# The sums of a row block of the project pass on DVE instead of POOL, and loads four row blocks ahead

## The chip, the core and the metric

The kernel runs on one core of a Trainium2 chip. The metric is the device time of one execution in microseconds, the median of several runs.

## The reference

Three layers in a row over 8 x 576 positions, 512 channels wide, all in fp32: a retention attention without softmax, a feed-forward layer with token mixing, and a gated feed-forward layer. In the middle one, with `x` the first layer's result:

```python
xt = x.transpose(0, 2, 1)
h = xt @ U @ V
u = x + h.transpose(0, 2, 1)
ch = np.maximum(u @ w_ch1, 0.0) @ w_ch2
return (u + ch).astype(np.float32)
```

`w_ch1` is 512 x 2048, `w_ch2` 2048 x 512. The last layer mixes each position with the one before it, and multiplies `relu(xk @ w_k)**2 @ w_v` with a sigmoid of `xr @ w_r`.

## The kernel before, in words

Each fp32 operand of a product is split into a high part (a copy on ACT, rounded to the fp32r type, L363) and a low part (the difference, on DVE, L364); a product is three matmuls: high by high, low by high, high by low.

The text is about the **project pass**, `relu(u @ w_ch1) @ w_ch2`. The nine column blocks of 512 positions are taken in four pairs (q = 0 to 3; the ninth is done apart behind them). The product of a pair is not made of eight block products but of seven (numbered 1 to 7) of sums and differences of blocks. Products 2, 1, 7 and 5 are made in a first half (h = 0), 6, 4 and 3 in a second (h = 1). Each half runs over eight **row blocks** (j = 0 to 7) of the hidden dimension, so there are 64 row blocks, counted by n. A row block is 24 matmuls in a first half (L404) and 18 in a second, each with 128 x 512 moving data, accumulated in four groups of PSUM banks (`ga` to `gd`).

What a row block goes through, by function:

- `load_item`: two tiles of 128 x 2 x 512, `ra` and `rb`, are loaded from DRAM by SP's queue. In a first half both hold four blocks of the hidden layer `hp`; in a second half `rb` is loaded again, and `ra` takes a half tile from the DRAM scratch `t`.
- `sums_item`: two operations of 128 x 512 (L345 and L346 in a first half, L349 and L350 in a second) make the sums in place. In a first half one sum is stored to `t` for the second half (L347).
- `split_item`: `sah` and `sbh` on ACT, `sal` and `sbl` on DVE.
- `products`: the matmuls. Behind the last row block of a half, `leave_group` takes the PSUM groups out: copies on ACT (L418, L440), additions on DVE (L424, L444), and it puts closures into the list `rest`: additions on POOL (L421, L432, L435, L454) and DVE (L448). These add the residual `u` (tiles `ur`, loaded by `load_rest`), and each result `x2` is then stored (L380), with a copy of its last column on ACT (L379).

`ra`, `rb`, `sbl` and `ur` share one pool of 16 buffers, `big2`; a new tile waits for the last reader of the one whose buffer it takes. On each engine instructions run in the order in which the code records them, and SP's queue is in order as well: a transfer that waits holds those behind it. The loop over n records the load of n+3, the sums of n+2, the split of n+1, the products of n, and then one closure of `rest` in a second half and two in a first.

Of the kernel before, what the change touches and what calls it, by code (L numbers as in the profile page):

```python
# [15 lines left out]
ALU = mybir.AluOpType  # L16
# [23 lines left out]
def retention_mixer_kernel(ctx: ExitStack, tc: tile.TileContext, io):  # L40
    nc = tc.nc

    consts = ctx.enter_context(tc.tile_pool(name="consts", bufs=1))
    big = ctx.enter_context(tc.tile_pool(name="big", bufs=35))
# [11 lines left out]
    def unit(pool, dt, nm):  # L56
        return pool.tile([128, 2, 512], dt, tag="unit", name=nm)

    def small(dt, nm):
        return sm.tile([128, 512], dt, tag="small", name=nm)  # L60
# [264 lines left out]
    ITEMS = [(q, h, j) for q in range(NB // 2) for h in range(2) for j in range(NF // 2)]  # L325
# [3 lines left out]
    def load_item(n):  # L329
        q, h, j = ITEMS[n]  # L330
        ra[n] = unit(big2, F32, f"ra{n}")
        rb[n] = unit(big2, F32, f"rb{n}")
        if h == 0:
            nc.sync.dma_start(ra[n], hp[q][:, j, 0:2])
        else:
            nc.sync.dma_start(ra[n][:, 0], t1_blk[q][:, j])
        nc.sync.dma_start(rb[n], hp[q][:, j, 2:4])
# [3 lines left out]
    def sums_item(n):  # L341
        q, h, j = ITEMS[n]
        a, b = ra[n], rb[n]
        if h == 0:
            nc.gpsimd.tensor_tensor(b[:, 0], b[:, 0], a[:, 1], op=ALU.subtract)  # L345
            nc.gpsimd.tensor_tensor(a[:, 1], a[:, 1], a[:, 0], op=ALU.subtract)  # L346
            nc.sync.dma_start(t1_blk[q][:, j], a[:, 1])  # L347
        else:
            nc.gpsimd.tensor_tensor(a[:, 0], b[:, 0], a[:, 0], op=ALU.subtract)  # L349
            nc.gpsimd.tensor_tensor(b[:, 1], b[:, 1], a[:, 0], op=ALU.subtract)  # L350

    def split_item(n):
        q, h, j = ITEMS[n]
        a, b = ra.pop(n), rb.pop(n)
        x = {}
        for nm, src, where in (("a", a, big), ("b", b, big2)):
            hi = unit(big, F32R, f"s{nm}h{n}")
            lo = unit(where, F32R, f"s{nm}l{n}")
            if h == 1 and nm == "a":
                src, hi_, lo_ = src[:, 0], hi[:, 0], lo[:, 0]  # L360
            else:
                hi_, lo_ = hi, lo
            nc.scalar.copy(hi_, src)  # L363
            nc.vector.tensor_tensor(lo_, src, hi_.bitcast(F32), op=ALU.subtract)  # L364
            x[nm] = hi, lo
        parts_of[n] = x
# [3 lines left out]
    ur = {}  # L370
    rest = []

    def load_rest(q, who):
        t, o = 2 * q + who % 2, who // 2
        ur[who] = unit(big2, F32, f"ur{t}_{o}")
        nc.sync.dma_start(ur[who], u_blk[t][:, 2 * o:2 * o + 2, :])

    def done_x2(t, o, x):
        nc.scalar.copy(edge[:, o, t:t + 1], x[:, BT - 1:BT])  # L379
        nc.sync.dma_start(x2_blk[t][:, o, :], x)  # L380

    def products(n):
        q, h, j = ITEMS[n]
        x = parts_of.pop(n)

        if h == 0:
            plan = {
                1: ("a", wp, 0, "a", 0), 2: ("b", wp, 1, "b", 1),
                5: ("d", wp, 2, "a", 1), 7: ("c", wp, 3, "b", 0),
            }  # L390
            seq_ = (2, 1, 7, 5) if j == 0 else (1, 7, 5, 2)
        else:
            plan = {6: ("a", wq, 2, "a", 0), 4: ("c", wq, 1, "b", 1), 3: ("d", wq, 3, "b", 0)}
            seq_ = (6, 4, 3)
        last = j == NF // 2 - 1
        for m in seq_:
            g, w, wi, nm, xi = plan[m]
            if h == 0 and j == 0:
                group[g] = [bank(2 * "abcd".index(g) + p, f"g{g}{q}_{p}") for p in range(2)]
            wh, wl = (v[:, wi] for v in w[j])  # L400
            xh, xl = (v[:, xi] for v in x[nm])
            for p in range(2):
                for i, (l, r) in enumerate(((wh, xh), (wl, xh), (wh, xl))):
                    nc.tensor.matmul(  # L404
                        group[g][p], l[:, col(p)], r,
                        start=(h == 0 and j == 0 and i == 0),
                        stop=(i == 2 and last),
                        skip_group_check=True,
                    )
            if last:  # L410
                for p in range(2):
                    leave_group(q, m, p, group[g][p])

    def leave_group(q, m, p, ps):
        if m in (1, 5, 7):
            to = {1: m1, 5: m5, 7: m7}[m]
            to[p] = small(F32, f"m{m}_{q}_{p}")
            nc.scalar.copy(to[p], ps)  # L418
        elif m == 2:
            def first(x=None):  # L420
                nc.gpsimd.tensor_tensor(m1[p], m1[p], ur[0][:, p], op=ALU.add)  # L421

            def out():
                nc.vector.tensor_tensor(m1[p], ps, m1[p], op=ALU.add)  # L424
                done_x2(2 * q, p, m1[p])

            rest.insert(p, first)
            rest.append(out)
            if p == 1:
                for i in range(2):  # L430
                    def add(i=i):
                        nc.gpsimd.tensor_tensor(m7[i], m7[i], m5[i], op=ALU.add)  # L432

                    def add_u(i=i):
                        nc.gpsimd.tensor_tensor(m7[i], m7[i], ur[3][:, i], op=ALU.add)  # L435

                    rest.extend([add, add_u])
        elif m == 6:
            u2[p] = small(F32, f"u2_{q}_{p}")
            nc.scalar.copy(u2[p], ps)  # L440
        else:
            who, nm = (2, "x21") if m == 4 else (1, "x12")
            x = small(F32, f"{nm}_{q}_{p}")
            nc.vector.tensor_tensor(x, ps, u2[p], op=ALU.add)  # L444
            t, o = 2 * q + who % 2, 2 * (who // 2) + p

            def add():
                nc.vector.tensor_tensor(x, x, ur[who][:, p], op=ALU.add)  # L448
                done_x2(t, o, x)

            rest.append(add)
            if m == 3:
                def last():
                    nc.gpsimd.tensor_tensor(m7[p], m7[p], u2[p], op=ALU.add)  # L454
                    done_x2(2 * q + 1, 2 + p, m7[p])

                rest.append(last)
# [3 lines left out]
    def load_hidden(p):  # L461
        hraw[p] = unit(big2, F32, f"hr{p}")
        nc.sync.dma_start(hraw[p], h_last[:, 2 * p:2 * p + 2, :])
# [3 lines left out]
    def split_hidden(p):  # L467
        r = hraw.pop(p)
        h, l = unit(big2, F32R, f"hh{p}"), unit(big2, F32R, f"hl{p}")
        nc.scalar.copy(h, r)  # L470
        nc.vector.tensor_tensor(l, r, h.bitcast(F32), op=ALU.subtract)
        hid[p] = h, l
# [71 lines left out]
    with ExitStack() as st:  # L544
# [228 lines left out]
        todo, ready = [], []  # L773
# [12 lines left out]
        def hidden(n, convert=True):  # L786
            for _ in range(n):
                if ready:
                    t, f = ready.pop(0)
                    m = bool(todo)  # L790
                    for part in range(3):
                        hidden_part(t, f, part)
                        mixes(1)
                    if convert and not m:
                        slot()
# [172 lines left out]
    big2 = ctx.enter_context(tc.tile_pool(name="big2", bufs=16, reuse_waits="tile"))  # L968
# [9 lines left out]
    def tick():  # L978
        ticks.append(0)
        slot(new=len(ticks) % 4 == 1)  # L980
# [3 lines left out]
        tick()  # L984
    ready.sort(key=lambda x: x[1] + 2 * (x[0] == NB - 1))
    while ready:
        if len(ready) in (6, 4, 2):
            load_item(3 - len(ready) // 2)
        if len(ready) in (3, 1):
            sums_item(len(ready) == 1)  # L990
        if len(ready) == 2:
            split_item(0)
        hidden(1, False)
        tick()
# [1 line left out]
    psum.append(ctx.enter_context(tc.tile_pool(name="psb", bufs=1, space=PSUM, reuse_waits="tile")))  # L996
    fetches = [(w, j) for w in later_weights for j in range(2)]
    for n, (q, h, j) in enumerate(ITEMS):
        if n + 3 < len(ITEMS):
            load_item(n + 3)  # L1000
        if n + 2 < len(ITEMS):
            sums_item(n + 2)
        if n + 1 < len(ITEMS):
            split_item(n + 1)
        if j in (3, 5):
            load_rest(q, ((0, 3), (2, 1))[h][j == 5])
        if n >= len(ITEMS) - 4:
            load_hidden(n - len(ITEMS) + 4)
        if n == len(ITEMS) - 1:
            split_hidden(0)  # L1010
        products(n)
        if waiting or going:
            tick()
        for _ in range(1 if h else 2):
            if rest and j < NF // 2 - 1:
                rest.pop(0)()
    for p in range(NF // 2):
# [167 lines left out]
```

## Time and profile before

| | before |
|---|---|
| median of 3 runs | 1450.95 us (1450.71 to 1454.95) |
| the profiled execution | 1453.18 us, its span 1451.4 us |
| TensorE busy in the span | 1396.6 us (96%), mean granted clock 0.984 |
| DVE, ACT, POOL busy | 713.3, 578.0, 518.0 us |
| project pass, four q blocks | 554.9 to 910.3 us |

The span is that of the core's instructions in the profiled execution; its own time, 1.8 us longer, is to be set beside the median of the runs. [...] The project pass is a quarter of the span, and the table's shares say little of it.

### The profile page before, as it was taken

What the parts mean: (1) busy time and instruction counts of PE and PEld (TensorE: products, weight loads), DVE (VectorE), ACT (ScalarE), POOL (GpSimd) and SP (SyncE); (2) the same over time, 40 slices, a digit from 0 to 9 for tenths busy, and PEclk for the clock granted to TensorE, in tenths of its full rate; (3) what the DMA queues carried; (4) which work ended last, traced back from release to release, by engine and by line L of the source; (5) the groups of instructions that cost most, each with busy time, mean ns of one, the idle gap of its engine ahead of it and who ended that gap; (6) DMA issues with size and microseconds to landing.
All of it is one profiled execution on the core that took longest, in us unless ns stands there. A gap on an engine that the chain in (4) does not pass through costs nothing. (4 is left out here: it accounts for less than half of the span.)

```text
span 1451.4 us, 25594 instructions
## 1 busy us (share of the span) xinstructions
PE 1396.6 (96%) x10332; PEld 1125.1 (78%) x10332; DVE 713.3 (49%) x1033; ACT 578.0 (40%) x1019; POOL 518.0 (36%) x375
## 2 busy tenths in 40 slices
PE   6899999999999999989989899999999999999998
PEld 4677878878788887867768677788888888888887
DVE  5872544445442557567676666544144144144240
ACT  4542333333333454433334343334344344344340
POOL 3340221122210558687786868120220220220220
PEclk8999999999999999989999999999999999999999
DMA  9756677676644567578676786771011011010000
GB/s 339 261 205 208 226 255 252 218 252 231 242 148 159 200 208 250 194 249 260 224 240 205 247 269 216 265 279 37 25 56 36 26 56 36 27 55 30 5 26 29
DMA packets 98951, 244.68 MB, mean 169 GB/s; under 512 B 12816, under 2 KB 19344, under 8 KB 98832
## 3 DMA queue, kind: packets, MB, share of 16 engines
q1 hardware_dynamic: 98832, 243.04, 49.1%
q8 instruction: 81, 1.33, 0.4%
q14 instruction: 38, 0.31, 0.1%
HBM read 158.07 MB, written 84.93 MB: 167 GB/s over the span
## 5 line engine op out<-in xcount | busy, mean ns | idle before, releaser
L1068 POOL TENSOR_TENSOR kl<-ks,kh 128x512 fp32r<-128x512 f32 x72 | 92.8, 1290 | 359.1 <-issue 241.8
L239 ACT ACTIVATE hs<-h 128x512 f32<-128x512 f32 x144 | 86.0, 598 | 242.1 <-PE h L233 237.6
L364 DVE TENSOR_TENSOR sal<-ra,sah 128x1024 fp32r<-128x1024 f32 (+1 forms) x64 | 92.3, 1443 | 108.2 <-ACT sah L363 100.2
L364 DVE TENSOR_TENSOR sbl<-rb,sbh 128x1024 fp32r<-128x1024 f32 x64 | 118.1, 1846 | 11.9 <-ACT sbh L363 11.9
L1098 DVE TENSOR_TENSOR o<-v,g 128x512 f32<-128x512 f32 x36 | 24.9, 691 | 187.2 <-PE v L1094 187.2
L1066 DVE SCALAR_TENSOR_TENSOR ks<-k,ka 128x512 f32<-128x512 f32 x72 | 49.6, 690 | 122.6 <-ACT ka L1064 67.7
L363 ACT CAST sah<-ra 128x1024 fp32r<-128x1024 f32 (+1 forms) x64 | 53.4, 835 | 119.6 <-POOL ra L346 71.1
L536 ACT CAST mh<-m 128x512 fp32r<-128x512 f32 x72 | 44.8, 623 | 115.7 <-DVE tp L529 82.7
L1094 PE MATMUL v<-wv_1u,kh 128*128 128x512 f32 x288 | 88.7, 389 | 0.0
L1094 PE MATMUL v<-wv_0u,kh 128*128 128x512 f32 x288 | 88.7, 389 | 0.0
L616 DVE TENSOR_TENSOR pm<-up,dtab 128x256 f32<-128x256 f32 x72 | 30.3, 421 | 108.5 <-PE up L629 90.4
L363 ACT CAST sbh<-rb 128x1024 fp32r<-128x1024 f32 x64 | 67.1, 1048 | 26.9 <-POOL rb L350 26.9
L1060 PE MATMUL k<-mh,wk_0u 128*128 128x512 f32 x288 | 71.6, 390 | 0.7 <-DMA wk_0u<-wk_kept 0.7
L1079 PE MATMUL r<-wru,mh 128*128 128x512 f32 x288 | 71.4, 389 | 0.0
L1060 PE MATMUL k<-mh,wk_1u 128*128 128x512 f32 x288 | 71.1, 389 | 0.0
L345 POOL TENSOR_TENSOR rb<-rb,ra 128x512 f32<-128x512 f32 x32 | 55.0, 1719 | 36.8 <-DMA rb<-hp 29.6
L1067 ACT CAST kh<-ks 128x512 fp32r<-128x512 f32 x72 | 44.5, 620 | 55.5 <-DVE ks L1066 55.5
L349 POOL TENSOR_TENSOR ra<-rb,ra 128x512 f32<-128x512 f32 x32 | 49.6, 1549 | 40.7 <-DMA rb<-hp 24.0
L1060 PEld LDWEIGHTS k<-mh,wk_0u 128*128 128x128 f32 x288 | 53.9, 188 | 12.4 <-ACT tp L523 1.1
L1064 ACT ACTIVATE ka<-k 128x512 f32<-128x512 f32 x72 | 43.0, 598 | 50.6 <-PE k L1060 41.7
L1079 PEld LDWEIGHTS r<-wru,mh 128*128 128x128 f32 x288 | 54.0, 188 | 11.6 <-ACT g L1083 0.4
L1094 PEld LDWEIGHTS v<-wv_0u,kh 128*128 128x128 f32 x288 | 54.1, 188 | 11.2
(196 smaller groups left out, 3451.8 us busy)
## 6 DMA issues: line engine op xcount, KB each, us to landing
hp<-hs SPq DMA_DIRECT2D x128, 256.0 KB, 2.9
rb<-hp SPq DMA_DIRECT2D x64, 512.0 KB, 6.0
qk<-in_qk SPq DMA_DIRECT2D x32, 512.0 KB, 4.6
kv<-in_kv SPq DMA_DIRECT2D x32, 512.0 KB, 6.0
ra<-hp SPq DMA_DIRECT2D x32, 512.0 KB, 5.2
ur<-ub SPq DMA_DIRECT2D x18, 512.0 KB, 6.9
x2l<-xb SPq DMA_DIRECT2D x18, 512.0 KB, 5.2
out<-o SPq DMA_DIRECT2D x36, 256.0 KB, 2.0
```

Of the source, the lines that this page charges most:

```text
L239: nc.scalar.activation(h, hps.pop((t, f)), AF.Relu)
L345: nc.gpsimd.tensor_tensor(b[:, 0], b[:, 0], a[:, 1], op=ALU.subtract)
L349: nc.gpsimd.tensor_tensor(a[:, 0], b[:, 0], a[:, 0], op=ALU.subtract)
L363: nc.scalar.copy(hi_, src)
L364: nc.vector.tensor_tensor(lo_, src, hi_.bitcast(F32), op=ALU.subtract)
L536: nc.scalar.copy(hk, m)
L1060: nc.tensor.matmul(ps, w.part(lo, k, fo), u[k // 2][:, k % 2, :], start=(i == 0), stop=(i == len(ops) - 1))
L1066: nc.vector.scalar_tensor_tensor(sq, ps, 0.0, a, op0=ALU.max, op1=ALU.mult)
L1067: nc.scalar.copy(kh, sq)
L1068: nc.gpsimd.tensor_tensor(kl, sq, kh.bitcast(F32), op=ALU.subtract)
L1079: nc.tensor.matmul(ps, x[k // 2][:, k % 2, io_], wr.part(lo, k), start=(j == 0), stop=(j == len(ops) - 1))
L1094: nc.tensor.matmul(ps, x[:, f % 2, io_], wv[f // 4].part(lo, f % 4), start=(j == 0), stop=(j == len(ops) - 1))
```

## The change

The two sums of a row block, 128 in all, are made on DVE instead of POOL. They are recorded where they were, so on DVE they now stand ahead of the split of the row block before. Loads are recorded four row blocks ahead. The residuals are loaded at j = 6 and 7 of a half instead of 3 and 5. In turn, the 16 additions of L448 go from DVE to POOL. `b` is split ahead of `a` in the first row block of each q block. Two closures of `rest` are taken up per row block in both halves, and the first four loads are recorded one step earlier or more in the pass ahead.

```diff
--- before.py
+++ after.py
@@ -342,18 +342,19 @@
         q, h, j = ITEMS[n]
         a, b = ra[n], rb[n]
         if h == 0:
-            nc.gpsimd.tensor_tensor(b[:, 0], b[:, 0], a[:, 1], op=ALU.subtract)
-            nc.gpsimd.tensor_tensor(a[:, 1], a[:, 1], a[:, 0], op=ALU.subtract)
+            nc.vector.tensor_tensor(b[:, 0], b[:, 0], a[:, 1], op=ALU.subtract)
+            nc.vector.tensor_tensor(a[:, 1], a[:, 1], a[:, 0], op=ALU.subtract)
             nc.sync.dma_start(t1_blk[q][:, j], a[:, 1])
         else:
-            nc.gpsimd.tensor_tensor(a[:, 0], b[:, 0], a[:, 0], op=ALU.subtract)
-            nc.gpsimd.tensor_tensor(b[:, 1], b[:, 1], a[:, 0], op=ALU.subtract)
+            nc.vector.tensor_tensor(a[:, 0], b[:, 0], a[:, 0], op=ALU.subtract)
+            nc.vector.tensor_tensor(b[:, 1], b[:, 1], a[:, 0], op=ALU.subtract)
 
     def split_item(n):
         q, h, j = ITEMS[n]
         a, b = ra.pop(n), rb.pop(n)
         x = {}
-        for nm, src, where in (("a", a, big), ("b", b, big2)):
+        two = (("a", a, big), ("b", b, big2))
+        for nm, src, where in two[::-1] if h == 0 and j == 0 else two:
             hi = unit(big, F32R, f"s{nm}h{n}")
             lo = unit(where, F32R, f"s{nm}l{n}")
             if h == 1 and nm == "a":
@@ -445,7 +446,7 @@
             t, o = 2 * q + who % 2, 2 * (who // 2) + p
 
             def add():
-                nc.vector.tensor_tensor(x, x, ur[who][:, p], op=ALU.add)
+                nc.gpsimd.tensor_tensor(x, x, ur[who][:, p], op=ALU.add)
                 done_x2(t, o, x)
 
             rest.append(add)
@@ -984,7 +985,7 @@
         tick()
     ready.sort(key=lambda x: x[1] + 2 * (x[0] == NB - 1))
     while ready:
-        if len(ready) in (6, 4, 2):
+        if len(ready) in (7, 5, 3, 1):
             load_item(3 - len(ready) // 2)
         if len(ready) in (3, 1):
             sums_item(len(ready) == 1)
@@ -996,14 +997,14 @@
     psum.append(ctx.enter_context(tc.tile_pool(name="psb", bufs=1, space=PSUM, reuse_waits="tile")))
     fetches = [(w, j) for w in later_weights for j in range(2)]
     for n, (q, h, j) in enumerate(ITEMS):
-        if n + 3 < len(ITEMS):
-            load_item(n + 3)
+        if n + 4 < len(ITEMS):
+            load_item(n + 4)
         if n + 2 < len(ITEMS):
             sums_item(n + 2)
         if n + 1 < len(ITEMS):
             split_item(n + 1)
-        if j in (3, 5):
-            load_rest(q, ((0, 3), (2, 1))[h][j == 5])
+        if j > 5:
+            load_rest(q, ((0, 3), (2, 1))[h][j - 6])
         if n >= len(ITEMS) - 4:
             load_hidden(n - len(ITEMS) + 4)
         if n == len(ITEMS) - 1:
@@ -1011,7 +1012,7 @@
         products(n)
         if waiting or going:
             tick()
-        for _ in range(1 if h else 2):
+        for _ in range(2):
             if rest and j < NF // 2 - 1:
                 rest.pop(0)()
     for p in range(NF // 2):
```

On SP's DMA queue, in the second half of the second q block (row blocks 24 to 31; `hp1` and `t11` are the hidden layer and the scratch of that q block, `ub` the residual, `xb` the results), before:

```order
L336 DMA ra27_8013<-t11_81 128x512 [waits DMAHW1_49,DVE_49]
L337 DMA rb27_8014<-hp1_76 128x1024 [waits DMAHW2_49,DVE_49,Pool_49]
L336 DMA ra28_8046<-t11_81 128x512 [waits DVE_49]
L337 DMA rb28_8047<-hp1_76 128x1024 [waits DMAHW4_49,Pool_49]
L336 DMA ra29_8079<-t11_81 128x512 [waits DMAHW5_49,DVE_49]
L337 DMA rb29_8080<-hp1_76 128x1024 [waits DMAHW6_49,DVE_49]
L380 DMA xb2_86<-m1_1_0_7983 128x512 [waits DMAHW7_49,DVE_49]
L336 DMA ra30_8114<-t11_81 128x512 [waits DMAHW0_49,PE_49]
L337 DMA rb30_8115<-hp1_76 128x1024 [waits DMAHW1_49,Activation_49]
```

And after the change:

```order
L337 DMA rb26_7926<-hp1_76 128x1024 [waits DMAHW1_49,DVE_49]
L377 DMA ur2_0_7939<-ub2_68 128x1024 [waits DMAHW7_49,DVE_49]
L336 DMA ra27_7965<-t11_81 128x512 [waits DMAHW4_49,DMAHW0_49,DVE_49]
L337 DMA rb27_7966<-hp1_76 128x1024 [waits PE_49]
L377 DMA ur3_1_7979<-ub3_69 128x1024 [waits DMAHW2_49,DVE_49]
L336 DMA ra28_8017<-t11_81 128x512 [waits DMAHW3_49,PE_49]
L337 DMA rb28_8018<-hp1_76 128x1024 [waits DVE_49]
L336 DMA ra29_8051<-t11_81 128x512 [waits DMAHW5_49,PE_49]
L337 DMA rb29_8052<-hp1_76 128x1024 [waits DMAHW6_49,DVE_49]
L381 DMA xb2_86<-m1_1_0_7987 128x512 [waits DMAHW7_49,DVE_49]
L381 DMA xb2_86<-m1_1_1_7989 128x512 [waits DMAHW0_49,DVE_49]
```

`rb28` waited for POOL, and so did what stands behind it; it waits for DVE after. The loads of a residual (`ur`) stand ahead of it, and two stores of results stand between the loads 29 and 30, which wait for DVE.

On DVE, about the same place (the border from the first to the second half of that q block), before:

```order
L364 TENSOR_TENSOR sal24_7970<-ra24_7884,sah24_7969 128x512 [waits PE_49,Activation_49]
L364 TENSOR_TENSOR sbl24_7974<-rb24_7885,sbh24_7973 128x1024 [waits DMAHW2_49,Activation_49]
L364 TENSOR_TENSOR sal25_8020<-ra25_7925,sah25_8019 128x512 [waits DVE_49,PE_49,Activation_49]
L364 TENSOR_TENSOR sbl25_8024<-rb25_7926,sbh25_8023 128x1024 [waits DMAHW6_49,Activation_49]
L364 TENSOR_TENSOR sal26_8053<-ra26_7963,sah26_8052 128x512 [waits DVE_49,PE_49,Activation_49]
L364 TENSOR_TENSOR sbl26_8057<-rb26_7964,sbh26_8056 128x1024 [waits DMAHW0_49,Activation_49]
L364 TENSOR_TENSOR sal27_8086<-ra27_8013,sah27_8085 128x512 [waits DVE_49,PE_49,Activation_49]
L364 TENSOR_TENSOR sbl27_8090<-rb27_8014,sbh27_8089 128x1024 [waits DMAHW2_49,DVE_49,Activation_49]
L424 TENSOR_TENSOR m1_1_0_7983<-gb1_0_7675,m1_1_0_7983 128x512
```

And after the change, with lines one further from L358 on:

```order
L365 TENSOR_TENSOR sal24_7972<-ra24_7847,sah24_7971 128x512 [waits PE_49,Activation_49]
L365 TENSOR_TENSOR sbl24_7976<-rb24_7848,sbh24_7975 128x1024 [waits Activation_49]
L349 TENSOR_TENSOR ra26_7925<-rb26_7926,ra26_7925 128x512 [waits DMAHW6_49,DMAHW5_49]
L350 TENSOR_TENSOR rb26_7926<-rb26_7926,ra26_7925 128x512 [waits DMAHW1_49,DVE_49]
L365 TENSOR_TENSOR sal25_8024<-ra25_7886,sah25_8023 128x512 [waits PE_49,Activation_49]
L365 TENSOR_TENSOR sbl25_8028<-rb25_7887,sbh25_8027 128x1024 [waits DMAHW7_49,Activation_49,Pool_49]
L349 TENSOR_TENSOR ra27_7965<-rb27_7966,ra27_7965 128x512 [waits DMAHW4_49,DMAHW1_49,DMAHW0_49]
L350 TENSOR_TENSOR rb27_7966<-rb27_7966,ra27_7965 128x512 [waits DVE_49]
L365 TENSOR_TENSOR sal26_8058<-ra26_7925,sah26_8057 128x512 [waits PE_49,Activation_49]
L365 TENSOR_TENSOR sbl26_8062<-rb26_7926,sbh26_8061 128x1024 [waits DMAHW2_49,Activation_49,Pool_49]
L425 TENSOR_TENSOR m1_1_0_7987<-gb1_0_7680,m1_1_0_7987 128x512
L425 TENSOR_TENSOR m1_1_1_7989<-gb1_1_7681,m1_1_1_7989 128x512
```

Between two splits there are two sums now, which wait for loads two row blocks ahead, and the low parts of the row blocks 25 and 26 wait for POOL, with L425 (L424 before) behind them.

On POOL, at that border, before:

```order
L349 TENSOR_TENSOR ra24_7884<-rb24_7885,ra24_7884 128x512 [waits DMAHW2_49,DMAHW1_49,PE_49]
L350 TENSOR_TENSOR rb24_7885<-rb24_7885,ra24_7884 128x512 [waits DVE_49,Pool_49]
L349 TENSOR_TENSOR ra25_7925<-rb25_7926,ra25_7925 128x512 [waits DMAHW6_49,DMAHW5_49,DVE_49]
L350 TENSOR_TENSOR rb25_7926<-rb25_7926,ra25_7925 128x512 [waits PE_49,Pool_49]
L349 TENSOR_TENSOR ra26_7963<-rb26_7964,ra26_7963 128x512 [waits DMAHW7_49,DMAHW0_49,DVE_49]
L350 TENSOR_TENSOR rb26_7964<-rb26_7964,ra26_7963 128x512 [waits DMAHW3_49,DVE_49,Pool_49]
L421 TENSOR_TENSOR m1_1_0_7983<-m1_1_0_7983,ur2_0_7816 128x512 [waits DMAHW4_49,Activation_49]
L349 TENSOR_TENSOR ra27_8013<-rb27_8014,ra27_8013 128x512 [waits DMAHW2_49,DMAHW1_49,DVE_49]
L350 TENSOR_TENSOR rb27_8014<-rb27_8014,ra27_8013 128x512 [waits DVE_49,Pool_49]
L421 TENSOR_TENSOR m1_1_1_7985<-m1_1_1_7985,ur2_0_7816 128x512 [waits Activation_49]
```

And after the change:

```order
L422 TENSOR_TENSOR m1_1_0_7987<-m1_1_0_7987,ur2_0_7939 128x512 [waits DMAHW2_49,DMAHW7_49,Activation_49,Pool_49]
L422 TENSOR_TENSOR m1_1_1_7989<-m1_1_1_7989,ur2_0_7939 128x512 [waits Activation_49,Pool_49]
L433 TENSOR_TENSOR m7_1_0_7997<-m7_1_0_7997,m5_1_0_8007 128x512 [waits DMAHW0_49,Activation_49]
L436 TENSOR_TENSOR m7_1_0_7997<-m7_1_0_7997,ur3_1_7979 128x512 [waits DMAHW2_49,Pool_49]
L433 TENSOR_TENSOR m7_1_1_7999<-m7_1_1_7999,m5_1_1_8009 128x512 [waits DMAHW1_49,Activation_49]
L436 TENSOR_TENSOR m7_1_1_7999<-m7_1_1_7999,ur3_1_7979 128x512 [waits Pool_49]
L449 TENSOR_TENSOR x21_1_0_8289<-x21_1_0_8289,ur2_1_8236 128x512 [waits DMAHW5_49,DMAHW4_49,DVE_49]
L449 TENSOR_TENSOR x21_1_1_8291<-x21_1_1_8291,ur2_1_8236 128x512 [waits DMAHW6_49,DVE_49]
L449 TENSOR_TENSOR x12_1_0_8299<-x12_1_0_8299,ur3_0_8271 128x512 [waits DMAHW0_49,DMAHW7_49,DVE_49,Activation_49]
L455 TENSOR_TENSOR m7_1_0_7997<-m7_1_0_7997,u2_1_0_8279 128x512 [waits Activation_49]
L449 TENSOR_TENSOR x12_1_1_8301<-x12_1_1_8301,ur3_0_8271 128x512 [waits DVE_49]
L455 TENSOR_TENSOR m7_1_1_7999<-m7_1_1_7999,u2_1_1_8281 128x512 [waits Activation_49,Pool_49]
```

The sums are gone from POOL. Six additions of one border follow each other, then the six of the next; the four of L449 (L448 before) are new there.

## Rows read from the trace of the kernel before

**Rows 1.** The page: the chain by engine; two groups of instructions with idle time and releaser.
```profile
PE 36%; POOL 3%; DMA 3%; issue 1%; DVE 1%; ACT 1%; SPq 0%; POOLq 0%; DVEq 0%
...
L345 POOL TENSOR_TENSOR rb<-rb,ra 128x512 f32<-128x512 f32 x32 | 55.0, 1719 | 36.8 <-DMA rb<-hp 29.6
...
L349 POOL TENSOR_TENSOR ra<-rb,ra 128x512 f32<-128x512 f32 x32 | 49.6, 1549 | 40.7 <-DMA rb<-hp 24.0
```

**Rows 2.** The chain of waits, a piece in the project pass: start, us, what.
```profile
805.82 5.39 DMA rb<-hp
...
811.38 2.09 POOL ra L349
```

**Rows 3.** Stretches: start and end, length, busy us (instructions) by engine, clock, DMA share, GB/s.
```profile
554.90:910.30 355.40, 325.61 (x1344) 256.77 (x1344) 233.14 (x162) 137.64 (x190) 272.70 (x161) 0.96 0.71 235
```

**Rows 4.** The chain of waits, a piece of the last pass.
```profile
1012.30 21.76 PE k L1060 x96
```

**Rows 5.** Waits of TensorE, 554 to 911 us: us in total, times, longest.
```profile
PE gb L404 <- ACT sbh L363: 7.7, 4, 2.0
PE ga L404 <- ACT sah L363: 7.0, 4, 2.1
PE gb L404 <- DVE sbl L364: 6.5, 4, 1.8
PE gc L404 <- DVE sbl L364: 5.8, 11, 0.6
PE ga L404 <- DVE sal L364: 4.7, 6, 1.7
```

**Rows 6.** Timeline of TensorE at the start of the third q block: idle before in brackets.
```profile
733.15 0.73 PE L404 MATMUL gb<-sbh,w2p 128*128 128x512 f32 x2 [1.94 <-ACT sbh L363]
735.68 0.50 PE L404 MATMUL gb<-sbl,w2p 128*128 128x512 f32 x1 [1.80 <-DVE sbl L364]
```

**Rows 7.** Timeline in the second half of the second q block, POOL and TensorE.
```profile
709.83 1.28 POOL L349 TENSOR_TENSOR ra<-rb,ra 128x512 f32<-128x512 f32 x1 [4.05 <-DMA rb<-hp]
...
711.81 0.73 PE L404 MATMUL ga<-sah,w2q 128*128 128x512 f32 x2 [1.33 <-ACT sah L363]
```

**Rows 8.** Two stretches, columns as in rows 3.
```profile
736.40:739.80 3.40, 3.40 (x10) 2.68 (x9) 3.40 (x5) 2.00 (x2) 2.66 (x3) 0.51 0.51 153
...
747.00:754.90 7.90, 7.90 (x37) 6.50 (x35) 6.69 (x6) 2.29 (x4) 4.46 (x3) 1.00 0.93 305
```

**Rows 9.** Timeline of DVE behind the project pass, POOL idle.
```profile
914.75 1.21 DVE L471 TENSOR_TENSOR hl<-hr,hh 128x1024 fp32r<-128x1024 f32 x1
915.89 0.68 DVE L448 TENSOR_TENSOR x<-x,ur 128x512 f32<-128x512 f32 x1
```

**Rows 10.** Timeline of POOL and DVE, 737 to 742 us.
```profile
737.43 1.29 POOL L345 TENSOR_TENSOR rb<-rb,ra 128x512 f32<-128x512 f32 x1 [0.66 <-DVE x L444]
...
737.94 1.86 DVE L364 TENSOR_TENSOR sal<-ra,sah 128x1024 fp32r<-128x1024 f32 x1
...
738.80 2.15 POOL L346 TENSOR_TENSOR ra<-ra 128x512 f32<-128x512 f32 x1
...
739.73 2.31 DVE L364 TENSOR_TENSOR sbl<-rb,sbh 128x1024 fp32r<-128x1024 f32 x1
```

**Rows 11.** Waits of SP's DMA queue, 554 to 911 us, columns as in rows 5.
```profile
SPq L347 <- POOL ra L346: 116.8, 31, 7.4
SPq L337 <- POOL m L421: 56.9, 4, 14.7
```

**Rows 12.** Timeline of SP's DMA queue in the second half of the second q block.
```profile
690.98 0.32 SPq L336 DMA_DIRECT2D ra<-t  x1
705.81 0.32 SPq L337 DMA_DIRECT2D rb<-hp  x1
```

**Rows 13.** Groups of instructions by line and shape, 554 to 911 us.
```profile
L424 DVE TENSOR_TENSOR m<-gb,m 128x512 f32<-128x512 f32 x8 | 5.4, 677 | 0.0
```

**Rows 14.** Transfers, 554 to 911 us: count, KB each, median us from issue to landing.
```profile
rb<-hp SPq DMA_DIRECT2D x62, 512.0 KB, 6.0
```

## Prediction

> **What bounds the kernel now.** The chain of waits comes first. Over the whole span TensorE holds 36% of it, POOL and the transfers 3% each [rows 1]; what is not TensorE lies in the project pass, and there the chain walks from the load of `rb` to the sums on POOL, to a copy on ACT, a subtraction on DVE and then TensorE, as in the pieces from 805.82 us on [rows 2]. So I look at that pass alone, 554.9 to 910.3 us [rows 3]: 355.40 us for 1344 matmuls. TensorE's own pace is read where nothing holds it, in the last pass: 96 matmuls in 21.76 us [rows 4], 0.2267 us each. At that pace the 1344 take 304.7 us, or 76.2 for each of the four q blocks. The difference is **50.7 us**, and the change can win no more than that and the wait just ahead of the window.
>
> What makes up the 50.7: TensorE's waits for split parts add up to 31.7 us [rows 5], some 30 of them inside the window. In time they stand in three kinds of place. The waits of `gb` are those at the start of each q block, four for `sbh` (7.7) and four for `sbl` (6.5): before the third, 1.94 and 1.80 [rows 6]. The four of `ga` for `sah` (7.0) stand in the middle of the second halves, one of them at 711.81 us [rows 7]. The other 10.5 us are many small ones. [...] The pass as a whole has 0.96 [rows 3], so about 0.04 x 355 = 14 us of full clock are missing, partly inside waits. The remainder, some 7 to 9 us, is the short refill after each wait.
>
> Why the parts are late has two answers. One is the pair POOL and DVE. Alone, a 128x1024 subtraction on DVE takes 1.21 us and a 128x512 addition 0.68 [rows 9]; a 128x512 sum on POOL takes 1.28 [rows 7]. Side by side they take turns: POOL's second sum starts at 738.80 and ends 1.15 us after DVE's `sal` has ended at 739.80, and `sbl`, from 739.73, ends 1.09 after that sum; so the one lasts 2.15, the other 2.31 [rows 10]. The other is the load. SP works in order, and four times it waits for POOL's L421, 56.9 us in all [rows 11]: between 690.98 and 705.81 it issues nothing [rows 12], because `rb28` takes over the buffer of a residual that POOL has not added yet. The load lands late, POOL's sum waits 4.05 us for it and TensorE 1.33 us [rows 7].
>
> **The change, part by part.** I count what the pair has to do for a q block, each instruction with two SBUF operands at its duration alone. Before: DVE 24 x 1.21 (splits) + 8 x 0.68 (half splits) + 4 x 0.68 (L448) = 37.2; POOL 32 sums and 8 additions, 40 x 1.28 = 51.2. Together 88.4 us, in a block that lasts 355.40/4 = 88.9. After: DVE 29.0 + 5.4 + 32 x 0.68 (sums) = 56.2; POOL 12 additions x 1.28 = 15.4. Together **71.6** in a block of 76.2. The gain is not in DVE's load (it rises by 19 us) but in the 32 sums that cost 1.28 on POOL and 0.68 on DVE. L424 and L444 have a PSUM operand and last 0.677 [rows 13]; six a block put 4.1 us more on DVE alone, 60.3.
>
> [...]
>
> **Sums ahead of the split.** On DVE the two sums of n+2 stand ahead of the split of n+1. A row block then asks 2 x 0.68 + 2 x 1.21 = 3.78 us of DVE against 24 x 0.2267 = 5.44 of TensorE in a first half, and 2 x 0.68 + 0.68 + 1.21 = 3.25 against 18 x 0.2267 = 4.08 in a second half: 1.66 and 0.83 to spare. The new wait is that splits queue behind sums that wait for a load; the load has three row blocks of time less their own work, 8.4 us in a second half (worked out at rival 3), against a median landing of 6.0 [rows 14]. I put it at nothing, covered by that lead; without the cover it is rival 3.
>
> **Loads four ahead, residuals at j = 6 and 7.** No `rb` load of a second half but the last waits for POOL's residual addition, so the holes of 14 us in SP go, with the kind of wait at 711.81. In exchange the split `sbl25` and `sbl26` (and their like) wait for POOL's L421 and L435, and the stores of `m1` stand in SP between loads 29 and 30 behind L424, which now waits behind `sbl26`. At the start of a next q block `sbl33` and the sum of `rb37` wait for POOL's L448. The stores of `t`, which wait 116.8 us in SP for POOL's L346 [rows 11], wait for the same sum on DVE. ACT's one-column copies L379 wait for POOL as they did for DVE and POOL before.
>
> **x additions on POOL.** 16 in all, 1.28 instead of 0.68: 0.6 x 4 = 2.4 us a block more on the pair; it is in the 71.6. They bunch: six POOL additions at each half's border.
>
> **What stays.** At a border the six hold the pair 6 x 1.28 = 7.7 us, and L424 or L444 add 1.35 or 2.7. Over the three row blocks in which they run DVE has 3 x 0.83 = 2.5 or 3 x 1.66 = 5.0 to spare. The shortfall is 6.5 into a second half, 5.4 into a next first half. DVE's lead on TensorE is about one row block, 4.1 to 5.4 us. So TensorE waits between 0 and 2.4 us (6.5 − 4.1) at a border; I take 1.2, between 6.5 − 5.4 = 1.1, the lead into a second half having been built at a first half's pace, and 5.4 − 4.1 = 1.3 the other way. 8 borders x 1.2 = 9.6. Behind two of them I set a stretch at the lower level of 3.40 us as in [rows 8], which loses 1.7: 3.4. Excess after: **13.0**. Bounds: 0 (the lead holds), and 8 x 2.4 + 8 x 1.7 = 33.
>
> Ahead of the first block stands one of the four waits for `sbh`, up to 2.0 us [rows 5]; earlier loads and `b` split first give 1.0 of it, between 0 and 2.0. The last pass has TensorE as its bound and stays.
>
> Sum: the profiled execution took 1453.2 us, span 1451.4. 1453.2 − 50.7 − 1.0 + 13.0 = 1414.5. It lay 2.2 above the median of the runs (1450.95), so **1412** for a median.
>
> **The rivals.**
> 1. *The pair stays the bound.* DVE's 60.3 and POOL's 15.4 are 75.7 of 76.2 if nothing overlaps. Today POOL also waits 29.6 + 24.0 us for loads in the pass [rows 1], 13.4 a block; if DVE inherits half, a block takes 82.4, some 83 with the refills. Excess 4 x 6.8 = 27: 1453.2 − 51.7 + 27 − 2.2 = 1426. For it: 88.4 of 88.9 today. Against: L424 and L444 need not queue, and POOL's wait for loads comes partly from SP's holes. It decides where DVE has no idle time left between borders.
> 2. *The borders' waits come back.* The additions on POOL now gate `sbl25`, `sbl26`, `sbl33` directly. The starts of q (7.7 + 6.5) and the four of `sah` (7.0) then keep their waits [rows 5] and the 14 us of clock behind them, with some 3 of refill; only the small ones go: 38 of excess, 1453.2 − 51.7 + 38 − 2.2 = 1437. Against: POOL is otherwise idle and starts at once.
> 3. *Slower: splits behind late loads.* Loads of n+4 go out only once n is split; from the split of n to that of n+3, which stands behind the sums of n+4, pass the landing, 3.25 us of DVE and two issues on SP of 0.32 [rows 12]. That is three row blocks, so one takes (landing + 3.89)/3, and from 12.24 − 3.89 = 8.4 us of landing on a second half is longer than TensorE's 4.08. With 13 us it is 5.63, 1.55 x 32 = 50 us in all, and the gain is lost; with 14 us 5.96, 60 us: 1453.2 − 51.7 + 60 − 2.2 = 1459. For it: the same bytes in less time raise the transfers' share from 0.71 [rows 3] to 0.71 x 355.4/304.7 = 0.83. Against: 6.0 now [rows 14], so it would have to double.
> 4. *No change:* the waits move to the loads' supply and the pass keeps its length, 1450.
>
> **How the numbers follow.** The forecast 0.71; rival 1 0.14, rival 2 0.07, rival 3 0.04, no change 0.04. The forecast's own range is 1400 (no excess: 1398.5) to 1421. For 8 in 10 I reach up to rival 1 and the upper bound of excess (1432): 1400 to 1432, which leaves out rivals 2 and 3 and a few chances below. A measurement of this kernel tells about 0.3%, 4.4 us: faster 0.92, same 0.04, slower 0.04.
>
> **What would show it.** Right: q blocks of 77 to 81 us in place of 88.9; DVE busy near 60 to 72 a block, POOL near 20; 128x512 sums on DVE at 0.68 except near borders, where they reach 1.8; SP without waits for L421 in front of loads; granted clock 0.98 or more over the pass; TensorE's remaining waits within three row blocks of a border. Wrong by rival 1: waits for `sal` and `sbl` spread over all row blocks and DVE without idle time. By rival 2: TensorE's waits for `sbl` of blocks 25, 26, 33, with POOL as what DVE waited for. By rival 3: DVE's sums waiting for `rb`, with landings above 8.4 us. The prediction fails downward if DVE's lead at borders is longer than a row block, upward if the load supply sets the pace.

## The result, and the profile after

The changed kernel takes 1406.63 us (median of 4 runs, 1404.54 to 1409.12), the one before in the same comparison 1452.22. The ratio is 0.9685, with a 95% interval of 0.966 to 0.971: 45.6 us less. The forecast was 1412, in a range of 1400 to 1432. The profiled execution of the changed kernel took 1404.54 us, the shortest of the four, and its span is 1402.8.

The page of the changed kernel, its chain by engine:

```profile
PE 96%; DVE 2%; DMA 1%; issue 1%; ACT 0%; SPq 0%; DVEq 0%; ACTq 0%
```

TensorE holds 96% of this chain, and it reaches back to the start. The line of [rows 1] cannot be set beside it: that chain, followed back from the end, breaks off at 792.7 us, so its shares are of the whole span but cover only the last 45% of it, and TensorE's 36% there are some 80% of what was followed. Its earliest piece (start, us, what):

```profile
792.72 0.01 POOL m L421
```

Stretches of the changed kernel (columns as in [rows 3]): the project pass, its first and its second q block, and a part of the first:

```profile
552.30:865.10 312.80, 307.94 (x1346) 252.97 (x1345) 266.61 (x280) 142.55 (x191) 78.85 (x49) 0.99 0.79 264
552.29:634.35 82.06, 78.37 (x337) 63.84 (x336) 69.96 (x75) 39.00 (x49) 20.08 (x13) 0.98 0.76 254
634.35:711.21 76.86, 76.47 (x337) 62.98 (x336) 66.65 (x71) 35.19 (x48) 19.43 (x13) 1.00 0.82 272
562.60:565.60 3.00, 2.99 (x7) 2.41 (x8) 2.90 (x3) 0.00 (x0) 1.09 (x1) 0.51 0.98 389
```

The pass begins at 552.3 us instead of 554.9 and lasts 312.80 us instead of 355.40. At TensorE's own pace it would be 304.7, so the excess fell from 50.7 to 8.1. The first q block takes 82.1, the three behind it 76.9 each. In the second, DVE is busy for 66.65 us and POOL for 19.43. The transfers' share rose from 0.71 to 0.79.

TensorE's waits in the pass, changed kernel, which answer to [rows 5] (us in total, times, longest):

```profile
PE ga L405 <- DVE sal L365: 4.4, 4, 3.2
PE gb L405 <- DVE sbl L365: 0.5, 1, 0.5
```

Of 31.7 us 4.9 are left, and 3.2 of them are one wait in the first q block. Behind it the granted clock is 0.51 for 3 us; it is 1.00 in the later blocks. Groups of the changed kernel by line and shape (count, busy us, mean ns, idle time ahead and its releaser):

```profile
L365 DVE TENSOR_TENSOR sbl<-rb,sbh 128x1024 fp32r<-128x1024 f32 x64 | 86.4, 1350 | 2.4 <-ACT sbh L364 2.2
...
L350 DVE TENSOR_TENSOR rb<-rb,ra 128x512 f32<-128x512 f32 x32 | 30.0, 936 | 1.1
...
L345 DVE TENSOR_TENSOR rb<-rb,ra 128x512 f32<-128x512 f32 x31 | 26.9, 867 | 4.1 <-DMA rb<-hp 4.1
L349 DVE TENSOR_TENSOR ra<-rb,ra 128x512 f32<-128x512 f32 x32 | 26.2, 820 | 4.2 <-DMA rb<-hp 4.2
...
L346 DVE TENSOR_TENSOR ra<-ra 128x512 f32<-128x512 f32 x31 | 24.8, 800 | 1.1
...
L449 POOL TENSOR_TENSOR x<-x,ur 128x512 f32<-128x512 f32 x14 | 20.2, 1456 | 108.2 <-DVE x L445 51.2 <-DMA ra<-hp 25.6 <-DMA rb<-hp 25.6
```

And two groups of the kernel before, of the same pass:

```profile
L364 DVE TENSOR_TENSOR sbl<-rb,sbh 128x1024 fp32r<-128x1024 f32 x64 | 118.1, 1846 | 11.9 <-ACT sbh L363 11.9
...
L346 POOL TENSOR_TENSOR ra<-ra 128x512 f32<-128x512 f32 x31 | 54.6, 1762 | 2.4
```

The four sums last 0.80 to 0.94 us in the mean on DVE, where they lasted 1.55 to 1.76 on POOL before, and `sbl` fell from 1846 to 1350 ns. The 53.6 us that POOL waited for loads [rows 1] became 8.3 on DVE. SP's waits in the pass:

```profile
SPq L347 <- DVE ra L346: 51.9, 31, 5.8
SPq L381 <- DVE m L425: 31.1, 8, 7.6
...
SPq L337 <- POOL x L449: 11.8, 3, 4.0
```

No load is held up by L422 (L421 before) any more, against 56.9 us in [rows 11]. The three that wait for L449 are those of `rb21`, `rb37` and `rb53`.

### The profile page after: what moved, and what is told of

Same layout as the page of the kernel before. It is cut to its first block, busy times and chain, and to the rows that moved or that the text cites. A ratio compares the mean times of both kernels' runs of the same rounds, so it can differ in the third digit from the quotient of the medians.

```text
span 1402.8 us, 25526 instructions
## 1 busy us (share of the span) xinstructions
PE 1378.8 (98%) x10332; PEld 1122.2 (80%) x10332; DVE 741.2 (53%) x1145; ACT 580.5 (41%) x1019; POOL 325.3 (23%) x263
## 4 chain that ended last, share of the span: by engine, by line
PE 96%; DVE 2%; DMA 1%; issue 1%; ACT 0%; SPq 0%; DVEq 0%; ACTq 0%
PE h L233 29%; PE k L1061 14%; PE v L1095 14%; PE r L1080 7%; PE gc L405 6%; PE ga L405 6%; PE gd L405 6%; PE gb L405 3%; PE up L605 2%; PE xn L705 2%; PE dn L658 1%; PE c L487 1%; PE c L486 1%; PE c L485 1%; PE up L630 1%; PE dn L646 1%
## 5 line engine op out<-in xcount | busy, mean ns | idle before, releaser
L365 DVE TENSOR_TENSOR sbl<-rb,sbh 128x1024 fp32r<-128x1024 f32 x64 | 86.4, 1350 | 2.4 <-ACT sbh L364 2.2
L365 DVE TENSOR_TENSOR sal<-ra,sah 128x1024 fp32r<-128x1024 f32 (+1 forms) x64 | 67.1, 1048 | 24.5 <-PE gd L405 16.5
L1061 PEld LDWEIGHTS k<-mh,wk_1u 128*128 128x128 f32 x288 | 54.1, 188 | 11.2
L1095 PEld LDWEIGHTS v<-wv_1u,kh 128*128 128x128 f32 x288 | 54.0, 188 | 11.2
```

The lines of the kernel that those rows point to most:

```text
L1061: nc.tensor.matmul(ps, w.part(lo, k, fo), u[k // 2][:, k % 2, :], start=(i == 0), stop=(i == len(ops) - 1))
L1095: nc.tensor.matmul(ps, x[:, f % 2, io_], wv[f // 4].part(lo, f % 4), start=(j == 0), stop=(j == len(ops) - 1))
```

## The experiments

All were compared with the kernel before on the same chip: twelve kernels, four runs each.

**The two halves of the change, each alone.** First only the sums, in the kernel before (the other three sums alike):

```diff
-            nc.gpsimd.tensor_tensor(b[:, 0], b[:, 0], a[:, 1], op=ALU.subtract)
+            nc.vector.tensor_tensor(b[:, 0], b[:, 0], a[:, 1], op=ALU.subtract)
```

> Only the sums go to DVE; loads stay three ahead, residuals stay at j = 3 and 5, the additions L448 stay on DVE. Theory A (the gain is the pair of DVE and POOL: 128 sums at 0.68 instead of 1.28 us, and POOL's residual additions no longer behind sums): most of the gain is here, 1410 to 1420 us. Theory B (the gain is the loads: earlier issue, no hole in SP): 1435 us or more, with TensorE's waits in the middle of the second halves still there.

It took 1425.40 us, ratio 0.9815 (0.9798 to 0.9832): 26.4 us less, of the 45.6 of the whole change. That is less than theory A wanted and more than B. What DVE waits for in it:

```profile
DVE rb L345 <- DMA rb<-hp: 30.5, 17, 3.1
DVE ra L349 <- DMA rb<-hp: 24.0, 12, 3.3
```

That is 54.5 us, as much as POOL waited for the same loads before. The wait for loads moved with the sums, whole; the sums' shorter time does not touch it. Then only the loads, with the sums left on POOL (the first four loads, ahead of the pass, go earlier as well):

```diff
-        if n + 3 < len(ITEMS):
-            load_item(n + 3)
+        if n + 4 < len(ITEMS):
+            load_item(n + 4)
...
-        if j in (3, 5):
-            load_rest(q, ((0, 3), (2, 1))[h][j == 5])
+        if j > 5:
+            load_rest(q, ((0, 3), (2, 1))[h][j - 6])
```

> Only the loads go four ahead and the residuals to j = 6 and 7; the sums stay on POOL. Theory A: SP's holes and the four waits in the middle of the second halves go (7 us and the lower clock behind them, about 12 in all), the waits at the starts of q stay: about 1440 us. Theory B: 1410 to 1420 us.

1432.39 us, ratio 0.9859 (0.9841 to 0.9877): 19.4 us. The two parts add up to 45.8, the whole is 45.6. So neither theory holds alone. That the sum comes out so well may be chance: both kernels leave out the three smaller edits (the additions of `x` on POOL, `b` first, two closures), and the undoings below do not add up as neatly. What is left with the sums on POOL is mainly one thing, 18.7 of TensorE's 24.7 us of waits; the timeline of the loads' kernel at the start of its third q block:

```profile
724.16 1.28 POOL L345 TENSOR_TENSOR rb<-rb,ra 128x512 f32<-128x512 f32 x1
...
725.51 1.26 POOL L346 TENSOR_TENSOR ra<-ra 128x512 f32<-128x512 f32 x1
726.74 1.26 POOL L435 TENSOR_TENSOR m<-m,ur 128x512 f32<-128x512 f32 x1
...
728.03 2.27 DVE L364 TENSOR_TENSOR sbl<-rb,sbh 128x1024 fp32r<-128x1024 f32 x1 [6.35 <-POOL m L435]
...
730.35 0.79 PE L404 MATMUL gb<-sbl,w2p 128*128 128x512 f32 x1 [5.65 <-DVE sbl L364]
```

`sbl` of the first row block takes over the buffer of a residual, POOL adds that residual behind three sums in its queue, and DVE waits 6.35 us for it and TensorE 5.65. There are three such waits (6.4, 5.7 and 6.6 us), one at each start of a further q block. POOL goes at its undisturbed 1.26 during this wait, so it is POOL's order that TensorE waits for, and not the pair's contention at that moment. The order has a second cause: a border leaves eight closures, of which a second half takes up one in each of seven row blocks, and this addition is the eighth, recorded in the next q block. The changed kernel takes up two. That was not tried with the sums on POOL, so how much of these waits is the sums and how much the one closure stays open. With its wait in it that q block lasts from 724.1 to 807.9, 83.8 us, though the pair still has the 88.4 us of work that I counted. That count of durations alone is therefore no floor for a block.

**The pair, tried by itself.** Work for POOL alone is added to the changed kernel; it is thrown away (`scr` is a tile made for it):

```diff
         if n + 1 < len(ITEMS):
             split_item(n + 1)
+            nc.gpsimd.tensor_copy(scr[:, 0:1], parts_of[n + 1]["a"][0][:, 0, 0:1].bitcast(F32))
+            nc.gpsimd.tensor_tensor(scr[:, 1:], scr[:, 1:], scr[:, 1:], op=ALU.add)
```

> The changed kernel with 63 further operations of 128x511 on POOL that add a scratch tile to itself, one behind each split's copy of sah (a copy of one column makes it wait for that); nothing waits for them, so it is work that is thrown away. If an operation on POOL that reads SBUF shuts DVE's two-operand operations out (the pair's sum rises from 71.6 by 16 x 1.28 = 20 us, to 92 in a block of 76.2): a block takes 80 to 92 us, 1420 to 1465 us. If the engines only share a rate or do not meet: 1405 to 1412 us.

And with a fill in place of the addition:

```diff
+            nc.gpsimd.memset(scr[:, 1:], 0.0)
```

> The same, but the 63 operations on POOL only write: they fill the scratch tile with a constant. Same queue, same copy of one column ahead of each. If reading SBUF is what shuts DVE out: 1405 to 1412 us, and DVE's operations beside them keep 0.68 and 1.21. If any operation on POOL does it: as long as with the additions, less the difference of their durations.

The additions cost 25.4 us (1432.03, ratio 0.9859, 0.9841 to 0.9876), the fills 2.9 (1409.48, ratio 0.9704, 0.9688 to 0.972). The timeline of the kernel with additions:

```profile
663.75 0.38 POOL L1008 COPY scr<-sah 128x1 f32<-128x1 f32 x1 [1.35 <-ACT sah L364]
664.09 1.03 POOL L1009 TENSOR_TENSOR scr<-scr 128x511 f32<-128x511 f32 x1
664.18 1.49 DVE L346 TENSOR_TENSOR ra<-ra 128x512 f32<-128x512 f32 x1
```

The 128x512 sum L346 lasts 1.49 us beside POOL's addition instead of 0.69. With fills:

```profile
653.98 1.21 DVE L365 TENSOR_TENSOR sbl<-rb,sbh 128x1024 fp32r<-128x1024 f32 x1
...
654.34 0.90 POOL L1008 COPY scr<-sah 128x1 f32<-128x1 f32 x1 [1.36 <-ACT sah L364]
...
655.12 0.68 DVE L345 TENSOR_TENSOR rb<-rb,ra 128x512 f32<-128x512 f32 x1
655.18 0.52 POOL L1009 MEMSET scr<- 128x511 f32 x1
...
657.63 1.22 DVE L365 TENSOR_TENSOR sbl<-rb,sbh 128x1024 fp32r<-128x1024 f32 x1
...
657.93 0.96 POOL L1008 COPY scr<-sah 128x1 f32<-128x1 f32 x1 [2.23 <-ACT sah L364]
...
658.77 0.68 DVE L345 TENSOR_TENSOR rb<-rb,ra 128x512 f32<-128x512 f32 x1
658.83 0.52 POOL L1009 MEMSET scr<- 128x511 f32 x1
```

Both of DVE's sums beside a fill here keep their 0.68. The fills are shorter (0.52 against the addition's 1.03 us), which alone would make them cost less; but these sums are not lengthened at all. What the fills' kernel still loses is not traced. DVE's `sbl` kept 1.21 and 1.22 us beside the one-column copies, though the copy reads; the copies lasted 0.90 and 0.96, and POOL's own additions stand behind them in its queue. The sizes are below what adding up gives: 16 additions a block would make it 92 us, and the pass lasts 339.8, 88.2 for the first block and 83.8 for each other. DVE's own busy time in the pass rose from 266.6 to 319.4, 0.84 us for each addition; with the fills it is 275.45.

**The lead of the loads and the residuals, undone in the changed kernel.** First the lead (of the first four loads, ahead of the pass, the fourth goes back into the loop):

```diff
-        if n + 4 < len(ITEMS):
-            load_item(n + 4)
+        if n + 3 < len(ITEMS):
+            load_item(n + 3)
```

> The changed kernel with loads three row blocks ahead in the loop; residuals stay at j = 6 and 7 and the first loads as early as there. If the fourth row block of lead covers nothing that three do not: 1405 to 1410 us. If it is what pays the sums' place ahead of the split: the chain landing 6 us, sums, split of two row blocks needs 4.08 x 2 = 8.2 in a second half against some 9.9: 1.7 us x 32, about 1460 us, with DVE waiting for rb.

1415.88 us, ratio 0.975 (0.9732 to 0.9767): 9.3 us more than the changed kernel, between the two expectations. The upper one counted double: 9.9 us pass over two row blocks, so the excess is 0.85 us a row block and not 1.7, which would give about 1434. DVE's waits for loads in it:

```profile
DVE ra L349 <- DMA rb<-hp: 17.6, 7, 4.0
DVE rb L345 <- DMA rb<-hp: 16.2, 12, 2.3
```

33.8 us against 8.3 in the changed kernel, and TensorE waits 1.1 to 1.8 us once in each second half and 0.6 to 0.9 behind the starts of q.

```diff
-        if j > 5:
-            load_rest(q, ((0, 3), (2, 1))[h][j - 6])
+        if j in (3, 5):
+            load_rest(q, ((0, 3), (2, 1))[h][j == 5])
```

> The changed kernel with the residuals loaded at j = 3 and 5 as before. If the late fetch takes POOL's additions off the loads' way (holes of SP come back, though POOL is empty and adds at once): 1415 to 1430 us with waits in the middle of halves. If an empty POOL is enough: 1405 to 1410 us.

1408.55 us, ratio 0.9697 (0.9678 to 0.9716): 1.9 us more, and the intervals overlap; in the profiles the pass lasts 315.7 against 312.6. No hole comes back: SP's loads wait for POOL 4.4 us in all. An empty POOL is nearly enough by itself. The closures, one per row block again in a second half:

```diff
-        for _ in range(2):
+        for _ in range(1 if h else 2):
```

> The changed kernel with one closure of additions and stores per row block in the second halves, as before, instead of two. If POOL, now empty, takes its additions as soon as their data is there whatever row block they are recorded in: 1405 to 1409 us. If the closures left over at the end of a half pile up at the next start of q: waits of sbl and sal in the row blocks behind it, 1411 us or more; the part of the gain that neither the sums alone nor the lead nor the late residuals explain (some 8 us) would then be here.

1407.36 us, ratio 0.9691 (0.9672 to 0.9709): no difference that the runs tell. The lead and the residuals undone one at a time are 9.3 + 1.9 = 11.2 us, and the sums alone stay 18.8 above the whole; about 7.6 are not found in any single undoing. Two edits that cover the same wait would hide so, each undone alone. One place where it may lie: in the kernel with the sums alone, where `a` is split first, TensorE waits 8.4 us for `sbl` at the four starts of q, and only 0.4 in the changed kernel with loads three ahead, where `b` is first. No kernel undid two edits of the changed one together.

**Smaller parts.** The additions of x back on DVE:

```diff
-                nc.gpsimd.tensor_tensor(x, x, ur[who][:, p], op=ALU.add)
+                nc.vector.tensor_tensor(x, x, ur[who][:, p], op=ALU.add)
```

> The changed kernel with the 16 additions of x back on DVE. If the pair's total counts (69.2 instead of 71.6 us a block): the three waits of 0.4 us behind the starts of q go, 1404 to 1406 us. If what counts is DVE's own queue at the border (four additions of 0.68 stand ahead of splits there): these waits grow to 1 us or more each, 1407 to 1412 us.

1405.55 us, ratio 0.9675 (0.966 to 0.9689). The three waits behind the starts of q are gone and these q blocks take 76.16 us, but the median does not tell it from the changed kernel: in the profile that pass began 2.3 us later, and what follows the pass took 1.1 us longer, with a wait of TensorE for `hl` of DVE. `a` ahead of `b` everywhere:

```diff
-        for nm, src, where in two[::-1] if h == 0 and j == 0 else two:
+        for nm, src, where in two:
```

> The changed kernel with a split ahead of b everywhere, as before. Product 2, the first of a q block, takes b: if the order is worth what the lead at that place allows (3.0 us of lead for sal and 4.1 for sbl in the changed kernel), the starts of q show no wait, only the first one does, by the 1.2 us of one split: 1406 to 1408.5 us. If b is late at each start of q as it was before: 1412 us or more.

1405.17 us, ratio 0.9675 (0.9659 to 0.9691): no difference. The later starts of q show no wait in their first row block either way; the first has 1.8 us for `sbl`, and in turn 1.9 instead of 3.2 in the row block behind.

**Sums ahead of the split, undone.**

```diff
-        if n + 2 < len(ITEMS):
-            sums_item(n + 2)
         if n + 1 < len(ITEMS):
             split_item(n + 1)
+        if n + 2 < len(ITEMS):
+            sums_item(n + 2)
```

> The changed kernel with the split of n+1 recorded ahead of the sums of n+2 in every row block. If what counts is only that DVE does first what TensorE wants first: as with the first two row blocks alone, 1400 to 1404 us. If sums ahead of the split are needed because ACT's copies wait for them (sah of n+2 then starts 1.2 to 2.4 us later, in a second half with 4.08 us a row block): waits for sal come back in second halves, 1408 to 1420 us.

1418.59 us, ratio 0.977 (0.9755 to 0.9784): 12 us slower than the changed kernel, by the second theory. DVE's waits in it:

```profile
DVE sal L365 <- ACT sah L364: 37.6, 32, 1.6
DVE sbl L365 <- ACT sbh L364: 11.2, 27, 0.5
```

48.8 us of DVE waiting for ACT's copies; the changed kernel has 10.0. The copies in turn wait for the sums just recorded, 95.8 us for L346 and L349 against 32.4 in the changed kernel. But in two row blocks of each q block the split may well go first:

```diff
+        ahead = n % 16 < 2
+        if ahead:
+            split_item(n + 1)
         if n + 2 < len(ITEMS):
             sums_item(n + 2)
-        if n + 1 < len(ITEMS):
+        if n + 1 < len(ITEMS) and not ahead:
             split_item(n + 1)
```

> The changed kernel, but in the first two row blocks of each q block the split of n+1 is recorded ahead of the sums of n+2. If DVE's order is what leaves the rest (3.2 us of wait in the second row block with the lower clock behind it, and three waits of 0.4 us): 1400 to 1404 us. If the split is late because of its own sum and the transfers, it moves nothing: 1405 to 1408 us.

1401.31 us (1399.78 to 1402.37), ratio 0.9649 (0.9633 to 0.9665): 5.3 us below the changed kernel. TensorE's waits in its pass:

```profile
PE ga L405 <- DVE sal L365: 1.2, 2, 0.8
PE gc L405 <- DVE sbl L365: 0.6, 1, 0.6
PE gb L405 <- DVE sbl L365: 0.5, 1, 0.5
```

2.3 us are left, all in the first three row blocks; the later q blocks take 76.16 us, TensorE's own pace. With the additions of x on DVE as well:

> The kernel with the split ahead in two row blocks of each q block, and also the 16 additions of x on DVE. Three of its four q blocks already go at TensorE's pace, as they do with the additions on DVE alone, so nothing is left for the second edit: 1400 to 1403 us. If the pair still costs something at the starts of q: 1398 to 1400 us.

1403.21 us, ratio 0.9661 (0.9647 to 0.9676): the intervals overlap, nothing more to win there.

## Why the prediction was right, point by point

What the change was to bring about came: the pass goes at TensorE's pace but for the borders and the first row blocks. That the pair's total was what had bound it is not shown (rival 1 below). The median was to be 1412 and is 1406.6. The profiled execution was to take 1414.5 us by the prediction's sum, and took 1404.5. The 10.0 us lie in three terms: what stays (4.9), ahead of the pass (1.7) and the last pass (3.4). Part of the 10.0 is the scatter of single executions, for the sum starts from one that lay 2.2 above its median, and the measured one lies 2.1 below.

- **The chain of [rows 1]** was misread: TensorE's 36% are not a share of a chain over the whole span, as it breaks off at 792.7 us. Nothing in the sum rests on it.
- **The ceiling of 50.7** held for the pass: TensorE's pace is the floor, and the kernel with the split ahead in two row blocks reaches it in three q blocks of four. The lower end, 1398.5, does not come out of the prediction's terms (1450.95 − 51.7 is 1399.3).
- **What stays, 13.0**, measured 8.1, and its make-up was wrong; that the term came so near is luck, since the borders gave 2.1 of the 13.0 and 5.9 come from a place that the sum did not have. The borders were to give 8 x 1.2 us with a clock of 0.51, as in [rows 8], behind two. Inside the pass there are seven, as the last half ends at the end of the pass. Into a second half there is no wait. `sal` of the last row block of a first half ends 5.5 us ahead of its first matmul and that of the next 6.1 (from the timelines), then 3.1, 0.9 and 0.8: the shortfall is 5.3, not 6.5, and DVE's lead 6.1, not 5.4. Into a first half the lead falls from between 2.7 and 3.6 us to 0.95 below zero in the third row block; that is a fall of 3.6 to 4.5 us, where 5.4 was forecast, from a lead smaller than the 4.1 that was. The result is three waits of 0.39, 0.7 each with the refill: from 645.23 to 646.57 three matmuls start in 1.34 us, which at 0.2267 each take 0.68, and the one behind the wait lasts 0.50 where those around it last 0.39 to 0.40. So q blocks take 76.9 or, the first, 82.1 us, and none lies in the 77 to 81 that were to show the prediction right. The timeline of the changed kernel behind the second start of q shows how:

```profile
639.42 2.27 POOL L455 TENSOR_TENSOR m<-m,u 128x512 f32<-128x512 f32 x1
640.47 1.78 DVE L345 TENSOR_TENSOR rb<-rb,ra 128x512 f32<-128x512 f32 x1
641.66 1.74 POOL L449 TENSOR_TENSOR x<-x,ur 128x512 f32<-128x512 f32 x1
642.28 1.67 DVE L346 TENSOR_TENSOR ra<-ra 128x512 f32<-128x512 f32 x1
643.36 1.74 POOL L455 TENSOR_TENSOR m<-m,u 128x512 f32<-128x512 f32 x1
643.87 2.31 DVE L365 TENSOR_TENSOR sal<-ra,sah 128x1024 fp32r<-128x1024 f32 x1
...
646.24 0.50 PE L405 MATMUL ga<-sal,w2p 128*128 128x512 f32 x1 [0.39 <-DVE sal L365]
```

POOL's additions and DVE's operations alternate, each of DVE's is some 1.1 us longer than alone, and `sal` is late by 0.39.

- **A wait that the sum had not**: 3.2 us in the second row block, which with the refill, the clock of 0.51 for 3 us and some small waits makes 5.9 of the 8.1. The timeline of the changed kernel:

```profile
554.91 1.22 DVE L345 TENSOR_TENSOR rb<-rb,ra 128x512 f32<-128x512 f32 x1
...
556.16 1.11 DVE L346 TENSOR_TENSOR ra<-ra 128x512 f32<-128x512 f32 x1
...
557.20 1.22 DVE L315 TENSOR_TENSOR w2p<-w2f,w2p 128x512 fp32r<-128x512 f32 x1
557.31 1.05 ACT L364 CAST sah<-ra 128x1024 fp32r<-128x1024 f32 x1 [3.19 <-DVE ra L346]
...
558.34 0.68 DVE L315 TENSOR_TENSOR w2q<-w2f,w2q 128x512 fp32r<-128x512 f32 x1
...
558.94 0.68 DVE L345 TENSOR_TENSOR rb<-rb,ra 128x512 f32<-128x512 f32 x1
...
559.66 0.69 DVE L346 TENSOR_TENSOR ra<-ra 128x512 f32<-128x512 f32 x1
...
560.27 2.29 DVE L365 TENSOR_TENSOR sal<-ra,sah 128x1024 fp32r<-128x1024 f32 x1
...
562.61 0.79 PE L405 MATMUL ga<-sal,w2p 128*128 128x512 f32 x1 [3.21 <-DVE sal L365]
```

The sums of row block 1 stand behind the first split; on DVE the last of the weights' parts (L315) and the sums of row block 2 come ahead of `sal`, which then meets POOL's own L315 and lasts 2.29 us instead of 1.21. The split ahead in these row blocks cuts it to 0.8, as shown.

- **Ahead of the pass** the gain was set at 1.0 between 0 and 2.0; the pass begins 2.7 earlier in the profile. The runs scatter here: in the changed kernel and the experiments that leave this place alone it begins between 552.3 and 555.1, so one profile does not tell the gain.
- **What follows the pass** was left at nothing and gave 3.4 us, which the ceiling did not count. TensorE's waits for `hh`, `hl` and a weight right behind the project pass, 0.9 + 0.9 + 0.7 us in the kernel before, are gone. `hh` waited 4.2 us on ACT for a residual addition in POOL's queue then; that POOL's empty queue releases it sooner is read from the two traces, and not tried alone.
- **The holes of SP** went, as said, and with them the waits in the middle of the second halves. The later residuals are not what it takes: with residuals at j = 3 and 5 and POOL empty of sums the holes stay away.
- **Sums ahead of the split at nothing**: no cost came of it in the steady state, but it was looked at as a cost only. The order is worth 12 us, for ACT's copies need the sums a row block early; in the first two row blocks of a q block it costs 5.
- **Loads four ahead**: landing is 5.7 us at the median, under the bound of 8.4, and rival 3 did not come. Three ahead costs 9.3.
- **Rival 1** did not come: blocks of 76.9 with DVE busy for 66.7 of them. The added additions show that the pair can bind: with 16 more of POOL's a block, the block takes 83.8. That 88.4 of 88.9 us stood for a full pair was a wrong reading: the same work fits in 83.8 with the loads early. One reason is in [rows 10]: an operation that started while the other ran ended only 1.09 to 1.15 us behind it, against 1.21 and 1.28 alone; that this is the whole of it is not shown. That L444 need not queue shows in the kernel before: at 646.37 us two of them, beside POOL's L346, took 1.27 us together, 0.68 or less each.
- **Rival 2**: `sbl25` and `sbl26` do wait for POOL's order by the program, but POOL, without sums, has added by then; such waits for POOL came only where the sums stayed on POOL.

What stays open is how the 26.4 us of the sums alone divide between the shorter operations and POOL's emptied queue: no kernel had the one without the other. The 7.6 us above stay open too.

## What to carry to other kernels

Before crediting a moved operation with its own time, look at what stood behind it in the old engine's queue: here the residual additions behind POOL's sums held buffers, and through them loads. A wait for a load moved here with its consumer (54.5 us), and it fell with the lead of the loads: 33.8 with three row blocks in the changed kernel, 8.3 with four. And where an engine keeps one order for all row blocks, look at the first ones of each block apart: the order that is right in the steady state cost 5 us there.

## What the runs showed of the hardware

An operation on POOL that only writes SBUF (0.52 us for 128x511) left two 128x512 sums of DVE at 0.68 us, while one that reads it (1.03 us) made a sum last 1.49. The two engines did not lose alike: in the fills' kernel a one-column copy on POOL, which reads, lasted 0.90 and 0.96 us beside DVE's `sbl` and ended 0.04 to 0.05 us behind it, while `sbl` kept 1.21 and 1.22. The durations of the pair alone, added up, overstated its need by some 5%: 88.4 us of them ran in 83.8.
